# Batch 0's first k load issued as two transfers, and one late row load issued by GpSimd

## The chip, the core and the metric

The kernel runs on one core of a Trainium2 chip. The core has five engines with their own instruction streams: PE (TensorE, matmuls and transposes through a matmul), DVE (VectorE), ACT (ScalarE), POOL (GpSimd) and SP (SyncE, which here only issues DMA transfers). Sixteen DMA engines carry the transfers; SP's transfers stand in one queue (q1 in the profile), GpSimd's in another (q0). The metric is the device time of one execution in microseconds (us).

## What is computed

Linear attention with cosine weights, followed by a gated feed-forward network. There are 8 batches, 8 heads, a sequence of 576 and a head size of 64; the attention's output is read as 4608 tokens of 512 values.

```python
def phi(x, c, s):
    r = np.maximum(x, 0.0)
    return np.concatenate([r * c, r * s], axis=-1)
q_p = phi(q, cos_w, sin_w); k_p = phi(k, cos_w, sin_w)
kv = np.einsum('bhsf,bhsd->bhfd', k_p, v)
z = np.sum(k_p, axis=2)
num = np.einsum('bhsf,bhfd->bhsd', q_p, kv)
den = np.einsum('bhsf,bhf->bhs', q_p, z)[..., None] + 1e-06
x = num / den                              # then laid out as (B * S, H * D)
rms = np.sqrt(np.mean(x * x, axis=-1, keepdims=True) + 1e-06)
xn = x / rms * rms_g
g = xn @ w_gate
out = (g / (1.0 + np.exp(-g)) * (xn @ w_val)) @ w_out
```

## The kernel before

The kernel goes batch by batch. The attention of a batch needs phi(k) and v for `kv` and `z`, then phi(q), transposed, for `num` and `den`; the result `xt` is normalised (`x_sq` squares and sums on ACT, GpSimd takes the power -1/2 into `rs` at L520, `x_norm` on DVE makes `xn` at L527), transposed into `xnT`, and goes through the feed-forward network in blocks of 512 tokens: for each of twelve slices of d_ff four matmuls with `wg` and four with `wv` (L556; in block 0 partly L643 and L658), a SiLU and a product into `hT`, then the matmuls with `wo` (L574). The blocks run in the order 0, 1, 2, 3, 4, 5, 6, 8, 7, where block 8 holds the rows left over from batches 1 to 7. While one block's network runs, the attention of later batches is fitted in between its steps: `at(blk, n, where, f, ...)` puts a call before, inside or after step n of block blk. The order of instructions on each engine is thus the order in which the program writes them; semaphores are placed by a framework.

**Tiles and queues.** Raw q, k and v come into a ring of five buffers named `raw` (L90 to L105). For batches 0 to 2 the rows of k and v lie as 64 x 9 tokens in a half of the partitions for each of two heads, and a dimension `hp` of four head pairs beside them (`kv_rows`). From batch 3 on (`wide`, L75) five tokens lie in a partition and 116 partitions are used. For batch 7 the last partition's row can't be read in one pattern with the others, so `load_kv` loads it separately: a single row, repeated five times, of 40 pieces of 64 values (L118 to L123). SP issues nearly all loads from batch 3 on, the DMA transposes and the output stores. GpSimd issues the loads of the start (q and v of batch 0 in `load_q0` and L213, the weights in L183 and L189) and of batches 1 and 2.

**The start.** SP first issues batch 0's k in two transfers (L149 to L153): tokens 0 to 3 of each partition's nine for all four head pairs (512 pieces of 256 values), then tokens 4 to 8 (512 pieces of 320). ACT issues the small `g4`. GpSimd builds an index table and constants, then issues the first half of q (`load_q0(0)`), v in two halves (`vv0`, L213), the second half of q, then the weights. PE runs ten fillers, matmuls on a zero tile (L598). Then:

```python
    for c in range(NC):
        k_phi(V, 0, c, 0)
        k_phi(A if c < 8 else V, 0, c, 1)
        z0_pe(c)
        if c < NDT:
            g_spread(psC[0], c)
    kv0_pe(0)
    kv0_pe(1)
```

`k_phi` makes phi(k) for token c of all four head pairs (DVE at L294, ACT at L292), `z0_pe` sums its columns on PE (L410), and `kv0_pe(hp)` makes k^T v of head pair hp (L430), which needs `vv0`. After that q is transposed on PE (L363), `kvzs` is copied out (L286, L288), and the chain `nd0_pe`, `nd_post`, `x_sq`, `x_norm`, `x_tr_pe` (L546) leads to the first feed-forward matmuls (L643).

**Semaphores of transfers.** SP's and ACT's transfers take eight semaphores in turn, GpSimd's eight others; a transfer waits until the transfer that used its semaphore before has landed.

Of the kernel before, what the change touches and what calls it, by code (L numbers as in the profile page):

```python
# [17 lines left out]
def kernel(  # L18
# [12 lines left out]
    B, H, S, D = q.shape  # L31
# [4 lines left out]
    HP = H // 2  # L36
    NC = S // 64
# [9 lines left out]
    V, A, G = nc.vector, nc.scalar, nc.gpsimd  # L47
# [22 lines left out]
    def kv_rows(src, b, hps):  # L70
        return src[b, 2 * hps[0] : 2 * hps[1], :, :].rearrange(
            "(hp hh) (s c) d -> (hh s) hp (c d)", hh=2, c=NC
        )

    def wide(b):  # L75
        return b > 2
# [4 lines left out]
    def kv_rows5(src, b, r0, r1):  # L81
        part = src[b, :, 0 : NC5 * (KP - 1), :].rearrange(
            "h (p c) d -> p h (c d)", c=NC5
        )[r0 : min(r1, KP - 1)]
        return bass.AP(part.tensor, part.offset, [[NC5 * D, r1 - r0]] + list(part.ap)[1:])
# [6 lines left out]
    def raw_tile(which, b):  # L92
        if (which, b) not in raw:
            t = ring.tile([P, H * NC5 * D], FP32, name="raw", tag="raw")
            raw[(which, b)] = t
        return raw[(which, b)]

    def raw_kv(which, b):
        t = raw_tile(which, b)
        if wide(b):  # L100
            return t[:, :].rearrange("p (h e) -> p h e", h=H)
        return t[:, 0 : HP * NC * D].rearrange("p (hp e) -> p hp e", hp=HP)
# [4 lines left out]
    def load_kv(which, b, hps=(0, HP), eng=nc.sync):  # L107
        src = k if which == "k" else v
        if not wide(b):
            return eng.dma_start(  # L110
                out=raw_kv(which, b)[:, hps[0] : hps[1], :], in_=kv_rows(src, b, hps)
            )
        last = KP if b < B - 1 else KP - 1
        for r0, r1 in ((0, KM), (KM, last)):
            eng.dma_start(
                out=raw_kv(which, b)[r0:r1, :, :], in_=kv_rows5(src, b, r0, r1)
            )
        if last < KP:  # L118
            eng.dma_start(
                out=raw_kv(which, b)[last:KP, :, :].rearrange("p h (c d) -> p h c d", d=D),  # L120
                in_=src[b, :, S - 1 : S, :].rearrange("h s d -> s h d").unsqueeze(2)
                .to_broadcast([1, H, NC5, D]),
            )  # L123
# [22 lines left out]

    g4 = one.tile([4, P], FP32, name="g4")
    nc.scalar.dma_start(out=g4[:, :], in_=moe_rms_g.rearrange("(t p) -> t p", p=P))
    for c0, c1 in ((0, 4), (4, NC)):  # L149
        nc.sync.dma_start(  # L150
            out=raw_kv("k", 0)[:, :, c0 * D : c1 * D],
            in_=kv_rows(k, 0, (0, HP))[:, :, c0 * D : c1 * D],
        )  # L153


# [67 lines left out]
    for i in range(3):  # L223
        m, e = math.frexp(left)
        part.append(math.ldexp(round(m * 256), e - 8))
        left -= part[i]
        G.memset(eps_rows[32 * i : 32 * i + 32, :], part[i] / 32)
    load_kv("k", 1, eng=G)
    load_w(wg, moe_w_gate, 8, NNT)

    def g_spread(bank, t):
# [12 lines left out]
        out=th[:, 0:NTAB], in0=fidx[:, :], scalar1=S - 1.0, scalar2=ang,  # L244
        op0=ALU.min, op1=ALU.mult,
    )
    for c0, c1, i0, less in ((0, 9, 0, 576.0), (13, 14, 13, 64.0), (19, NTAB, 13, 64.0)):
        V.tensor_scalar(
            out=th[64:128, c0:c1], in0=fidx[64:128, i0 : i0 + c1 - c0],
# [4 lines left out]
        out=th[:, NTAB : 2 * NTAB], in0=th[:, 0:NTAB], scalar1=math.pi / 2.0,  # L254
# [4 lines left out]
        out=sel[:, :, :], in_=ident[0:4, 0:4].unsqueeze(2).to_broadcast([4, NDT, P])  # L259
# [437 lines left out]
    x_sq(0, 1)  # L697
    load_q(1, eng=G)
    load_kv("v", 1, eng=G)
    x_norm(0, 0, (0, HALF))  # L700
    x_norm(0, 0, (HALF, DM))
# [63 lines left out]
    for j in range(4):  # L765
# [3 lines left out]
        if j < 2:  # L769
            at(0, 10 + j, "pe", q_tr_pe, 1, j, bank)  # L770
            at(0, 10 + j, "pre", q_tr_evac, V, 1, j, bank)
    at(0, 8, "post", load_kv, "k", 2, (0, HP), G)
    at(0, 9, "post", v_cast, G, 1, (0, 2))
    at(0, 10, "pre", v_cast, V, 1, (2, 4))
# [184 lines left out]
```

## Time and profile before

| | us |
|---|---|
| median of three runs (322.75, 322.88, 323.72) | 322.88 |
| the profiled execution | 322.91 |
| its span, first to last instruction | 321.1 |
| PE busy | 313.6 |
| DVE busy | 185.4 |
| ACT busy | 165.8 |
| GpSimd (POOL) busy | 40.5 |

The granted clock of PE was 1.0 over the whole span. The DMA engines are busy through most of it: of 40 equal slices the first 29, to 233 us, each have a mean busy share of 0.5 or more. SP's queue carried 41.25 MB, GpSimd's 12.13 MB.

Landing times, median from issue: 5.5 us for the 640 KB of batch 0's k; 6.6 and 8.3 us for the two halves of batch 0's q; 7.2 us for the halves of its v; 13.8 to 20.0 us for groups of weights.

How to read the lines below: in the timeline and in the chain of waits the first two columns are start and length in us; the bracket at the end of a timeline line is the time for which the engine was idle before the instruction and what ended that. In lists of waits the numbers are the total in us, how many, and the longest.

### The profile page before, as it was taken

To read this page: it belongs to the slowest core of one execution; us is meant where nothing else is said; L and a number is where in the kernel's file an instruction comes from. 1 tells how busy PE (TensorE), PEld (TensorE's weight loads), DVE (VectorE), ACT (ScalarE), POOL (GpSimd) and SP (SyncE) were. 2 spreads that over 40 slices of the span, in tenths; PEclk is the share of its full clock that TensorE was granted. 3 is DMA by queue.
4 is the path that set the end of the run, shared out by engine and by line. 5 is a ranking of instruction groups with operands and counts; after the bars stand their busy time and mean duration, and the time that the engine had idled before them with its cause. 6 is when DMAs were issued, how large, how long until landed. Compare 5 with 4: busy or idle time off the path is not lost.

```text
span 321.1 us, 6023 instructions
## 1 busy us (share of the span) xinstructions
PE 313.6 (98%) x2274; PEld 162.4 (51%) x2310; DVE 185.4 (58%) x382; ACT 165.8 (52%) x322; POOL 40.5 (13%) x79
## 2 busy tenths in 40 slices
PE   7999999999999999999999999999999999999996
PEld 2689564544454445444544445544544444444444
DVE  7976977668457773777457644781676034204410
ACT  5766756754574466554744575446543233223321
POOL 9771211002001100010001100100011000000000
PEclk9999999999999999999999999999999999999999
DMA  7999999788999999999799959995522500041002
GB/s 232 239 270 269 282 329 227 201 183 190 223 226 211 187 263 187 221 247 182 162 186 230 197 163 200 197 217 163 99 59 41 116 33 0 0 102 31 1 35 98
DMA packets 80092, 53.76 MB, mean 167 GB/s; under 512 B 52235, under 2 KB 74047, under 8 KB 80063
## 3 DMA queue, kind: packets, MB, share of 16 engines
q1 hardware_dynamic: 73110, 41.25, 62.1%
q0 software_dynamic: 6944, 12.13, 15.5%
q8 instruction: 18, 0.29, 0.4%
q14 instruction: 12, 0.09, 0.1%
q10 hardware_dynamic: 8, 0.00, 0.0%
HBM read 37.83 MB, written 9.44 MB: 147 GB/s over the span
## 4 chain that ended last, share of the span: by engine, by line
PE 94%; DMA 2%; DVE 1%; issue 1%; POOL 1%; ACT 0%; POOLq 0%; ACTq 0%
PE psC L574 27%; PE psV L556 27%; PE psG L556 26%; PE psV L643 2%; PE psA L449 2%; DMA vv<-in_v_dram 2%; PE psG L574 2%; PE psG L643 2%; PE psA L387 2%; PE psA L394 1%; PE psA L474 0%; PE psV L363 0%; PE psG L430 0%; PE psC L546 0%; POOL raw L135 0%
## 5 line engine op out<-in xcount | busy, mean ns | idle before, releaser
L571 DVE TENSOR_TENSOR hT<-psV,sg 128x512 bf16<-128x512 f32 x99 | 68.2, 689 | 96.5 <-PE psV L556 64.1
L556 PE MATMUL psV<-xnT,wv 128*128 128x512 bf16 x344 | 89.6, 379 | 0.7 <-issue 0.2
L570 ACT ACTIVATE sg<-psG 128x512 f32<-128x512 f32 x99 | 58.6, 592 | 60.8 <-PE psG L556 52.7
L556 PE MATMUL psG<-xnT,wg 128*128 128x512 bf16 x337 | 88.5, 379 | 0.7 <-issue 0.2
L574 PE MATMUL psC<-wo,hT 128*128 128x512 bf16 (+1 forms) x400 | 88.4, 376 | 0.4
L574 PEld LDWEIGHTS <-hT 128*128 128x128 bf16 x456 | 43.1, 98 | 47.7
L556 PEld LDWEIGHTS <-wv 128*128 128x128 bf16 x400 | 39.0, 98 | 46.8
L556 PEld LDWEIGHTS <-wg 128*128 128x128 bf16 x400 | 37.0, 98 | 39.9 <-DVE xnT L288 0.2
L520 POOL TENSOR_TENSOR rs<-ms,mhalf 128x1 f32<-128x1 f32 x36 | 20.5, 570 | 193.9 <-ACT scr L515 193.7
L286 ACT COPY osb<-psC 128x512 f32<-128x512 f32 x32 | 18.7, 585 | 49.9 <-PE psC L574 46.1
L515 ACT ACTIVATE scr<-xt 128x513 bf16<-128x513 f32 x36 | 22.8, 635 | 23.3 <-DVE xt L499 22.3
L527 DVE SCALAR_TENSOR_TENSOR xn<-xt,rs,gb 128x512 bf16<-128x512 f32 (+1 forms) x37 | 26.9, 730 | 9.9 <-POOL rs L520 9.9
L292 ACT ACTIVATE kp<-raw,tab 128x256 bf16<-128x256 f32 (+2 forms) x51 | 28.8, 607 | 2.4 <-DMA raw<-in_k_dram 2.4
L499 DVE TENSOR_TENSOR xt<-psA,rec 128x512 f32<-128x512 f32 x36 | 24.9, 691 | 1.2
L292 ACT ACTIVATE qp<-raw,tab 128x512 bf16<-128x512 f32 (+1 forms) x36 | 23.3, 666 | 1.2 <-DMA raw<-in_q_dram 1.1
L294 DVE TENSOR_SCALAR kp<-raw,tab 128x256 bf16<-128x256 f32 (+2 forms) x53 | 20.1, 428 | 0.5 <-DMA raw<-in_k_dram 0.5
L294 DVE TENSOR_SCALAR qp<-raw,tab 128x512 bf16<-128x512 f32 (+1 forms) x34 | 15.3, 463 | 4.7 <-DMA raw<-in_q_dram 4.7
L449 PEld LDWEIGHTS <-qpT 128*128 128x128 bf16 x224 | 10.6, 97 | 6.6
L556 PE MATMUL psV<-xnT_tail,wv 128*128 128x512 bf16 x48 | 12.3, 379 | 0.1
L556 PE MATMUL psG<-xnT_tail,wg 128*128 128x512 bf16 x46 | 12.0, 379 | 0.1
L288 DVE CAST vv<-raw 116x1280 bf16<-116x1280 f32 (+1 forms) x13 | 11.1, 857 | 1.3 <-DMA raw<-in_v_dram 1.3
L449 PE MATMUL psA<-kvzs,qpT 128*128 128x65 bf16 x224 | 11.4, 193 | 0.0
(102 smaller groups left out, 177.7 us busy)
## 6 DMA issues: line engine op xcount, KB each, us to landing
out_dram<-osb SPq DMA_DIRECT2D x27, 256.0 KB, 2.3
raw<-in_q_dram SPq DMA_DIRECT2D x6, 1024.0 KB, 9.1
raw<-in_k_dram SPq DMA_DIRECT2D x5, 1120.0 KB, 8.8
raw<-in_v_dram SPq DMA_DIRECT2D x5, 1120.0 KB, 9.4
raw<-in_k_dram POOLq DMA_DIRECT2D x2, 1152.0 KB, 19.2
raw<-in_v_dram POOLq DMA_DIRECT2D x2, 1152.0 KB, 15.7
out_dram<-osb SPq DMA_DIRECT2D x17, 128.0 KB, 2.6
wg<-in_moe_w_gate_dram POOLq DMA_DIRECT2D x3, 512.0 KB, 13.8
```

The source lines that it names most:

```text
L286: A.copy(out=o, in_=i)
L292: A.activation(out=out_ap, in_=in_ap, func=AF.Relu, scale=scale)
L294: eng.tensor_scalar(out=out_ap, in0=in_ap, scalar1=scale, scalar2=0.0, op0=ALU.mult, op1=ALU.max)
L449: nc.tensor.matmul(heads[:, g, hp, :], lhsT=qpT[:, h, j * P : (j + 1) * P], rhs=kvzs[b][:, g, hp * E : (hp + 1) * E], start=True, stop=True,)
L499: V.tensor_tensor(out=xt[:, 0:DM].rearrange("p (hp g d) -> p g hp d", g=2, d=D), in0=heads[:, :, :, 0:D], in1=rec[:, :, :].unsqueeze(3).to ...
L515: A.activation(out=scr[:, :], in_=xt[:, 0 : DM + 1], func=AF.Square, scale=1.0 / math.sqrt(DM), accum_out=ms[:, :],)
L520: G.tensor_tensor(out=rs[:, :], in0=ms[:, :], in1=mhalf[:, :], op=ALU.pow)
L527: V.scalar_tensor_tensor(out=xn_of[(b, j)][:, c], in0=x_of[(b, j)][:, c], scalar=rs_of[(b, j)][:, :], in1=gb[:, c], op0=ALU.mult, op1=ALU. ...
L556: nc.tensor.matmul(bank[:, cols[0] : cols[1]], lhsT=w[:, t, n * P : (n + 1) * P], rhs=x[:, t, cols[0] : cols[1]], start=(t == 0), stop=(t ...
L570: A.activation(out=sg[:, :], in_=g[:, 0:TB], func=AF.Silu)
L571: V.tensor_tensor(out=hT[:, n, :], in0=v[:, 0:TB], in1=sg[:, :], op=ALU.mult)
L574: nc.tensor.matmul(bank[:, 0 : cols[1] - cols[0]], lhsT=hT[:, n, j * P : (j + 1) * P], rhs=wo[:, n, cols[0] : cols[1]], start=(n == 0), st ...
```

## The change

Batch 0's first k transfer (tokens 0 to 3) becomes two transfers on the same queue, SP's: head pairs 0 and 1, then head pairs 2 and 3, with 256 pieces each. The transfer of tokens 4 to 8 stays as it is, behind them. Users of tokens 0 to 3 wait for both transfers. In `load_kv` the single-row load at the end of batch 7 is issued by GpSimd instead of SP where it is a load of k; that of v stays on SP.

```diff
         if last < KP:
-            eng.dma_start(
+            (G if which == "k" else eng).dma_start(
                 out=raw_kv(which, b)[last:KP, :, :].rearrange("p h (c d) -> p h c d", d=D),
                 in_=src[b, :, S - 1 : S, :].rearrange("h s d -> s h d").unsqueeze(2)
                 .to_broadcast([1, H, NC5, D]),
...
-    for c0, c1 in ((0, 4), (4, NC)):
+    for hps, c0, c1 in (((0, 2), 0, 4), ((2, HP), 0, 4), ((0, HP), 4, NC)):
         nc.sync.dma_start(
-            out=raw_kv("k", 0)[:, :, c0 * D : c1 * D],
-            in_=kv_rows(k, 0, (0, HP))[:, :, c0 * D : c1 * D],
+            out=raw_kv("k", 0)[:, hps[0] : hps[1], c0 * D : c1 * D],
+            in_=kv_rows(k, 0, hps)[:, :, c0 * D : c1 * D],
         )
```

In the built program SP's stream has the two transfers of 256 pieces, then the one of 512. GpSimd's stream has batch 7's row between its 27th and its 28th `rs` of 36, after waits on semaphores of older transfers. The semaphores of SP's transfers stand one place further round from the start to batch 7's k load, and as before from there on. ACT and DVE wait for one more semaphore ahead of their first `k_phi`. The order of PE's, DVE's and ACT's instructions does not change.

## The prediction

> **What bounds the kernel now.** I read the shares of busy time, then the chain of waits, then the first 17 us in order of time, then the DMA queues in short windows. TensorE (PE) is busy 98% of the span, and over the stretch from 16 to 60 us the waits of PE name almost nothing:
>
> ```profile
> PE 313.6 (98%) x2274; PEld 162.4 (51%) x2310; DVE 185.4 (58%) x382; ACT 165.8 (52%) x322; POOL 40.5 (13%) x79
> PE psV L556 <- issue: 0.2, 1, 0.2
> ```
>
> So from about 17 us on nothing but the number of matmuls sets the end, and whatever moves the start of that stretch moves the end by as much. The chain of waits (start, length, what) shows what the start hangs on:
>
> ```profile
> 2.01 1.01 POOL raw L135
> 3.02 6.81 DMA vv<-in_v_dram
> 9.82 0.04 issue
> 9.87 0.71 PE psG L430 x36
> ...
> 12.56 0.43 DVE kvzs L288
> ...
> 16.96 0.28 PE psC L546 x2
> ```
>
> The reader is to see that batch 0's k is not on it. The chain goes through GpSimd's issue of q, then through the first half of batch 0's v (`vv0`), which lands at 3.02 + 6.81 = 9.82; then the k^T v products (L430) start. How near is k? The timeline says:
>
> ```profile
> 0.72 1.01 SPq L150 DMA_DIRECT2D raw<-in_k_dram  x2
> ...
> 5.04 3.42 ACT L292 ACTIVATE kp<-raw,tab 128x256 bf16<-128x256 f32 x8 [2.38 <-DMA raw<-in_k_dram]
> 5.06 3.79 DVE L294 TENSOR_SCALAR kp<-raw,tab 128x256 bf16<-128x256 f32 x10 [0.55 <-DMA raw<-in_k_dram]
> ...
> 8.91 0.39 PE L410 MATMUL psV<-kp,ones 64*128 64x512 bf16 x1
> ...
> 9.87 0.71 PE L430 MATMUL psG<-vv,kp 64*128 64x64 bf16 x36 [0.57 <-DMA vv<-in_v_dram]
> ```
>
> The first k transfer releases ACT and DVE at 5.04, phi(k) ends at 5.06 + 3.79 = 8.85, the column sums (L410) at 8.91 + 0.39 = 9.30, and PE then waits 0.57 us for v. So k has 0.57 us to spare, yet it is not free: both share the DMA engines. The queues' packets in the windows 1.6 to 2.6, 2.6 to 3.4, 3.4 to 5.4 and 5.4 to 6.3 us (q1 is the queue of SP, q0 that of GpSimd; the last two lines are one window; packets, MB, share of 16 engines):
>
> ```profile
> q1 hardware_dynamic: 63, 0.06, 51.1%
> ...
> q1 hardware_dynamic: 199, 0.20, 84.4%
> ...
> q1 hardware_dynamic: 674, 0.78, 108.3%
> ...
> q0 software_dynamic: 51, 0.21, 71.0%
> q1 hardware_dynamic: 120, 0.13, 45.0%
> ```
>
> These are all 1,056 packets of k (512 + 512 pieces, 32 semaphore writes). GpSimd's queue moves nothing before 5.4, although its q was issued at 1.95, and starts as SP's queue runs dry. So v lands when the engines have done k, then q, then v: if k leaves them sooner, v may land sooner. And k starts slowly: 63 packets in the first window against 337 per us (674 in 2.0 us) in the third.
>
> **The change part by part.** The profiled execution took 322.91 us: a span of 321.1 and 1.81 around it. That is 0.03 above the median of the runs (322.88), so I sum against 322.91.
>
> *The first transfer in two.* Bytes and pieces stay (2 x 256 of 1 KB). SP issues one more transfer; its two issues now start 0.52 us apart (0.72 and 1.24), so the second half of k (640 KB) is issued at 1.76 instead of 1.24. That costs nothing while its packets stand behind the first half's: 262 of those 512 were served by 3.4 us, 1.6 us later than the new issue; the first of the second half came at 3.73 in the trace's packet records. Were that cover gone, it would cost up to 0.52. Sixteen more semaphore writes, one per engine, of about 10 ns each in those records: 0.01 us.
>
> The unknown term is the slow start. From the first packet at 1.85 to 3.4 us, 262 packets took 1.55 us; at 337 per us they would have taken 0.78. So at best the cut saves 0.77 us; at worst the queue pauses once for an issue, +0.5. What do rows say of size? The 63rd piece of this load came 1.88 us after its issue; in the four larger k and v loads of some 900 pieces (issued at 66.9, 74.5, 98.4 and 126.6 us) it came after 1.98 to 2.24. About 400 pieces more cost 0.10 to 0.36 us, so 256 fewer might save 0.06 to 0.23. I take -0.2, near the upper of the two since here 16 engines each get 16 pieces instead of 32 before the next transfer feeds them. Both transfers are needed before phi(k) starts, so nothing is won by the first alone.
>
> How much arrives at the end? If q and v follow k without a gap, all of it: phi(k), q, v, the q for j = 2 and 3, and the weights all stand in the same engines' order. If GpSimd's queue could not have begun before 5.4 anyway, none. I take all of the -0.2; the second is a rival.
>
> *One more wait.* ACT and DVE now wait for two transfers before their first phi(k). A semaphore instruction lasts 17 to 28 ns where SP has them (L115). It lies in the 0.57 us that k has to spare: nothing.
>
> *The tiny load.* The last row of batch 7's k, 40 pieces, leaves SP and joins GpSimd's instructions between the 27th and the 28th `rs` (L520):
>
> ```profile
> 183.76 0.55 POOL L520 TENSOR_TENSOR rs<-ms,mhalf 128x1 f32<-128x1 f32 x1 [5.25 <-ACT scr L515]
> 199.85 0.55 POOL L520 TENSOR_TENSOR rs<-ms,mhalf 128x1 f32<-128x1 f32 x1 [15.55 <-ACT scr L515]
> ...
> 195.02 0.80 SPq L119 DMA_DIRECT2D raw<-in_k_dram  x1
> 195.99 1.66 SPq L346 DMA_TRANSPOSE qpT<-qp  x1
> ```
>
> GpSimd idles 15.55 us there. Its issues take 0.74 to 1.08 us (L110, L183, L135), so the load goes out by about 185.4 if its semaphores, those of loads several batches older, are met. Behind it stands only the `rs` at 199.85, then DVE's `xn`. With the slowest landing of a GpSimd load on the page, 20.0 us, it is there by 205.4; phi of batch 7 starts at 213.43. Nothing. Without the cover, each us past 199.85 would hold back `rs`, and DVE behind it. SP gains 0.97 us (195.02 to 195.99) for the transposes behind it, but PE waits for none of them: nothing. From the start to there, SP's transfers use the semaphore one place further round the eight; each still waits for the transfer eight before it: nothing.
>
> **Sum:** -0.2 + 0.01 + 0 = -0.19, rounded -0.2; 322.91 - 0.2 = 322.7 us.
>
> **The rivals.**
>
> *A. GpSimd's queue is not ready before 5.4.* For it: no packet of q0 sooner, 2.4 us after its issue ended at 3.02. Against: its start falls just when SP's queue runs dry. Then v lands at 9.82 as before: 322.9.
>
> *B. The whole slow start goes.* With engines fed in half the time, the 0.77 us vanish, and the first packet comes sooner too: it comes 1.13 us after the issue here, and 0.84 after the issue of an output store of 128 pieces. -0.77 - 0.29 = -1.06: 321.85. For it: the engines' share is 51% and 84% where it could be 100%. Against: the weak dependence on size above, and some first packets last 0.4 to 0.8 us, which looks like memory and not supply.
>
> *C. GpSimd's q slips between k's pieces (slower).* The second half of k is issued 0.52 us later; should GpSimd's packets come first or by turns, its 640 KB, which took some 1.9 us (4.4 to 6.3), would take twice that and land near 8.6 instead of 1.24 + 5.5 = 6.74. Six of DVE's ten phi(k) (0.38 us each) follow, 2.3 us, and then the last column sums, 0.45 us (8.85 to 9.30): 11.35, where L430 starts at 9.87 now. +1.5: 324.4. It decides once that half lands after 7.1 (9.87 - 0.45 - 2.3). For it: q0 has work issued from 1.95 on. Against: it did not slip in at the boundary between the two transfers before.
> The Trainium skill ("DMA: Bandwidth & Descriptors", Queues, rings and completion order) has each engine take turns between the queues that have work, packet by packet. By that rule C is what happens as soon as q0 is ready before k is through; the trace has no such turn before 5.4, so by the rule q0 was not ready, which speaks for A.
>
> *D. Each transfer pays its fixed part in line (slower).* Issue to first packet is 1.13 us and last packet to release about 0.5 (4.52 to 5.04); a third transfer paying them over again lands k's second half 1.6 later, at 8.35: L430 at 11.1, +1.2: 324.1. Against: the second transfer's packets now begin while the first's still run, at 389 GB/s without a gap.
> The Trainium skill (same page, Anatomy of one DMA) gives a fixed cost of about 2.0 us per transfer on GpSimd's path; paid in line it would add an estimated 2.0 to the landing. The trace disagrees for SP's queue: 640 KB landed 1.7 us after the 512 KB released their users.
>
> *E. PE falls to half pace (slower).* The first fillers (512 columns) follow each other 0.42 to 0.43 us apart until about 4.5 us, L410's matmuls of as many columns at 8.02 to 8.9 us 0.22 apart. If a longer gap before 17 us brought that pace back for the same 3.3 us, it costs 1.65: 324.6. Against: PE's longest wait once started is 0.6 us, and the forecast shortens the first one.
>
> **How the numbers follow.** Forecast 0.36, A 0.16, B 0.26, C 0.12, D 0.04, E 0.06. About 0.3% (1 us) is what a measurement of this kernel can tell from no change. Forecast and A are within it: 0.52; B is faster: 0.26; C, D and E are slower: 0.22. The likeliest gives 322.7, its own range 322.2 to 323.3 (from 322.91, the bounds -0.77 and +0.5 of the slow start, each drawn in by 0.1). To hold 8 in 10 the range reaches to B on one side and towards C on the other: 321.7 to 324.3.
>
> **What would show it.** Right: ACT's first phi(k) at about 4.85, v landing and the first L430 near 9.65, more than 63 packets in 1.6 to 2.6; GpSimd's L119 near 184.3. A: k earlier, L430 still at 9.87. B: phi(k) near 4.0. C: packets of q0 before q1 is through, and DVE waiting for k between its phi(k). E: L643 twice as long from 17 us. Wrong altogether: any new wait of PE after 30 us, above all behind `xn` near 200 us.

## The result, and the profile after

The changed kernel takes 327.4 us (median of 5 runs, 327.02 to 327.89), the kernel before 323.06 us beside it (5 runs, 322.75 to 326.27): a ratio of 1.0113, with a 95% interval of 1.0065 to 1.0162. The change makes the kernel slower by some 4.3 us. The forecast was 322.7 us (321.7 to 324.3).

The profiled execution took 327.09 us with a span of 325.28 (before: 322.91 and 321.13), so the 4.15 us lie inside the span. From the page of the changed kernel, first the shares of busy time, then a line of the 40 slices:

```profile
PE 318.6 (98%) x2310; PEld 164.1 (50%) x2310; DVE 185.2 (57%) x382; ACT 165.7 (51%) x322; POOL 40.7 (13%) x80
...
PEclk9599999999999999999999999999999999999999
```

PE is busy for 318.6 us instead of 313.6, with the same instructions (2310 records against 2274: some matmuls are missing from the trace of the kernel before, as both have 2310 weight loads), and in the second slice (8 to 16 us) it was granted half its clock. That is where to look. The chain of waits of the changed kernel, in the first 14 us (start, length, what):

```profile
1.73 8.34 DMA raw<-in_k_dram
10.07 0.02 issue
10.09 0.52 ACT kp L292
10.61 0.04 issue
10.65 0.58 PE psC L410
...
12.97 0.97 PE psG L430 x36
```

Before, the chain went through v. Now it goes through k, and only one of its three transfers: the third, issued at 1.73, lands at 10.07. The timeline of the changed kernel shows both sides of the change:

```profile
0.72 1.48 SPq L150 DMA_DIRECT2D raw<-in_k_dram  x3
...
4.50 1.71 ACT L292 ACTIVATE kp<-raw,tab 128x256 bf16<-128x256 f32 x4 [1.83 <-DMA raw<-in_k_dram]
4.52 1.60 DVE L294 TENSOR_SCALAR kp<-raw,tab 128x256 bf16<-128x256 f32 x4
...
10.09 1.71 ACT L292 ACTIVATE kp<-raw,tab 128x256 bf16<-128x256 f32 x4 [3.89 <-DMA raw<-in_k_dram]
10.09 1.66 DVE L294 TENSOR_SCALAR kp<-raw,tab 128x256 bf16<-128x256 f32 x6 [3.98 <-DMA raw<-in_k_dram]
...
10.65 0.58 PE L410 MATMUL psC<-kp,ones 64*128 64x512 bf16 x1 [2.60 <-ACT kp L292]
...
12.74 1.21 PE L430 MATMUL psG<-vv,kp 64*128 64x64 bf16 x36
```

The halves did what they were cut for: phi(k) begins at 4.50 instead of 5.04. But ACT and DVE, which went through all of k in one stretch before, stop after tokens 0 to 3 and wait 3.89 and 3.98 us for tokens 4 to 8. PE stands still for 2.60 us, and L430 starts at 12.74 instead of 9.87. Where the packets were can be read from the DMA queues in the windows 1.6 to 2.6, 2.6 to 3.4, 4.0 to 5.1, 6.3 to 7.5 and 7.5 to 9.7 us of the changed kernel (packets, MB, share of 16 engines):

```profile
q1 hardware_dynamic: 110, 0.11, 52.7%
...
q1 hardware_dynamic: 315, 0.31, 108.7%
...
q1 hardware_dynamic: 112, 0.14, 71.9%
...
q0 software_dynamic: 78, 0.32, 72.8%
q1 hardware_dynamic: 56, 0.07, 15.7%
...
q0 software_dynamic: 275, 0.37, 85.1%
q1 hardware_dynamic: 174, 0.21, 28.4%
```

The same query over 4.0 to 5.1 us of the kernel before:

```profile
q1 hardware_dynamic: 359, 0.43, 107.4%
```

In the first two windows the changed kernel is ahead: 110 and 315 packets against 63 and 199. Its first 512 pieces end at 3.96 us in the packet records, against 4.52. Then, where the kernel before goes on at full pace, SP's queue falls to a third, 0.14 MB in 1.1 us instead of 0.43. From 6.3 us most of the engines' time goes to GpSimd's q and v. By the semaphores, to which each of the sixteen engines adds one when its share is done, eight engines finish their share of the third transfer between 5.97 and 7.12, about as before (6.02 to 6.74); the other eight only between 9.03 and 10.07.

PE's pace, from windows of the changed kernel (length, then busy time and instructions of PE, PEld, DVE, ACT, POOL; then PE's granted clock, DMA share, GB/s):

```profile
10.00:12.70 2.70, 2.05 (x10) 0.96 (x12) 2.61 (x9) 2.61 (x7) 1.12 (x4) 0.50 1.15 291
12.70:16.00 3.30, 3.30 (x64) 2.96 (x60) 2.15 (x5) 1.35 (x4) 1.74 (x3) 0.50 1.23 216
16.00:21.50 5.50, 5.40 (x100) 3.64 (x98) 4.43 (x12) 4.59 (x12) 2.41 (x4) 1.00 1.24 207
```

By the clock's records PE is at half clock from 9.15 to 15.97, for 6.83 us: this begins while PE still waits (8.05 to 10.65), and goes on for 5.3 us behind the wait. The first feed-forward matmul (L643) starts at 21.49 instead of 17.31. So the account is: L430 later by 2.87; from L430 to L643 8.75 us instead of 7.44, another 1.31; from L643 to the end 303.79 instead of 303.82. Together 2.87 + 1.31 - 0.03 = 4.15, the whole difference.

The moved row, on GpSimd in the changed kernel:

```profile
187.94 0.55 POOL L520 TENSOR_TENSOR rs<-ms,mhalf 128x1 f32<-128x1 f32 x1 [5.25 <-ACT scr L515]
188.62 0.64 POOL L119 DMA_DIRECT2D raw<-in_k_dram  x1
204.04 0.56 POOL L520 TENSOR_TENSOR rs<-ms,mhalf 128x1 f32<-128x1 f32 x1 [14.79 <-ACT scr L515]
```

It is issued 0.1 us after the `rs` ahead of it ends, and GpSimd still idles 14.79 us behind it.

### The profile page after: what moved, and what is told of

The parts are those of the page before. It is cut to its first block, busy times and chain, and to the rows that moved or that the text cites. A ratio compares the mean times of both kernels' runs of the same rounds, so it can differ in the third digit from the quotient of the medians.

```text
span 325.3 us, 6063 instructions
## 1 busy us (share of the span) xinstructions
PE 318.6 (98%) x2310; PEld 164.1 (50%) x2310; DVE 185.2 (57%) x382; ACT 165.7 (51%) x322; POOL 40.7 (13%) x80
## 4 chain that ended last, share of the span: by engine, by line
PE 94%; DMA 3%; ACT 1%; SPq 0%; DVE 0%; POOL 0%; issue 0%; ACTq 0%
PE psC L574 27%; PE psV L556 27%; PE psG L556 27%; DMA raw<-in_k_dram 3%; PE psV L643 2%; PE psA L449 2%; PE psG L574 2%; PE psG L643 2%; PE psA L387 2%; PE psA L394 1%; PE psC L410 1%; PE psV L363 1%; ACT qp L292 0%; PE psA L474 0%; PE psC L546 0%; ACT qpT L286 0%
## 5 line engine op out<-in xcount | busy, mean ns | idle before, releaser
L556 PE MATMUL psG<-xnT,wg 128*128 128x512 bf16 x352 | 90.3, 379 | 0.0
L294 DVE TENSOR_SCALAR qp<-raw,tab 128x512 bf16<-128x512 f32 (+1 forms) x34 | 16.3, 492 | 4.3 <-DMA raw<-in_q_dram 4.3
(103 smaller groups left out, 184.3 us busy)
```

Source lines behind the costliest of these rows:

```text
L294: eng.tensor_scalar(out=out_ap, in0=in_ap, scalar1=scale, scalar2=0.0, op0=ALU.mult, op1=ALU.max)
L556: nc.tensor.matmul(bank[:, cols[0] : cols[1]], lhsT=w[:, t, n * P : (n + 1) * P], rhs=x[:, t, cols[0] : cols[1]], start=(t == 0), stop=(t ...
```

## The experiments

Times are medians. The kernel before was run beside each group and took 323.0 (24 runs), 323.2 (32 runs) and 323.18 (15 runs) for the three groups that follow. Each diff is an excerpt. It is against the kernel before, but for `gap_filled` and `gpsimd_late`, where it shows what is added to the changed kernel; where only the head of the loop over k's transfers is shown, the lines under it are those of the change. In `split_only`, `tiny_first` and `tiny_mid` the row of batch 7 stays on SP; in all others GpSimd issues it as in the change, which only the diff of `row_only` shows.

### The two parts alone, and a third transfer that is not a split

`split_only`: the split without the row.

```diff
-    for c0, c1 in ((0, 4), (4, NC)):
+    for hps, c0, c1 in (((0, 2), 0, 4), ((2, HP), 0, 4), ((0, HP), 4, NC)):
```

> The first k load in two, batch 7's row left on SP's queue. If the split is the cause (theory 1): as slow as the changed kernel, 326.5 to 328, the second half of k (tokens 4 to 8) landing near 10 us, phi(k) of token 4 starting near 10 and PE's clock halved in one stretch before 17 us. If the moved row is the cause, or its shift of the semaphores' order (rival): near 323, phi(k) without a stop in the middle.

Measured: 326.76 us, ratio 1.0115 (1.0096 to 1.0134). The timeline of `split_only` has the same break:

```profile
4.29 1.71 ACT L292 ACTIVATE kp<-raw,tab 128x256 bf16<-128x256 f32 x4 [1.63 <-DMA raw<-in_k_dram]
...
9.67 1.71 ACT L292 ACTIVATE kp<-raw,tab 128x256 bf16<-128x256 f32 x4 [3.67 <-DMA raw<-in_k_dram]
```

The split alone makes the loss.

`row_only`: the row on GpSimd without the split.

```diff
-            eng.dma_start(
+            (G if which == "k" else eng).dma_start(
```

> Only batch 7's row moved to GpSimd. Theory 1: no change, 322.7 to 323.5, since GpSimd idles 15 us there. Rival (the row is the cause): 326 to 328.

Measured: 323.23 us, ratio 1.001 (0.9998 to 1.0023). The row is worth nothing that can be measured.

`tiny_first` and `tiny_mid`: k's two transfers as before, with a load of 2 KB that nothing uses issued by SP ahead of both, or between them. In each, k's last transfer is the third in SP's queue and is issued about 0.5 us later than before, as in the change.

```diff
+    gx = one.tile([4, P], FP32, name="gx")
+    nc.sync.dma_start(out=gx[:, :], in_=moe_rms_g.rearrange("(t p) -> t p", p=P))
     for c0, c1 in ((0, 4), (4, NC)):
```

> The kernel before, with one more load of 2 KB that nobody uses issued on SP's queue ahead of k's two. Three transfers on the queue, the last issued 0.5 us later, as in the changed kernel, but a transfer of 512 pieces stands right ahead of the last. Theory 2a (the third transfer, or its later issue, is what starves the last one): the last lands near 10 us, 326 to 328. Theory 2b (the last transfer starves because the short ones ahead of it end before its pieces are ready): its start is covered until about 4.3 us, k lands about 0.5 later than before (5.5 and 7.3), 323 to 323.9.

> The same 2 KB load issued between k's two transfers. The last transfer is third and 0.5 us later, with 512 pieces ahead of it. Theory 2a: it lands near 10 us, 326 to 328. Theory 2b: covered until about 3.7 us, as before; lands by 7, 322.7 to 323.6.

Measured: `tiny_first` 324.08 us, ratio 1.0037 (1.0016 to 1.0059); `tiny_mid` 323.14 us, ratio 1.0005 (0.9993 to 1.0016). In neither does phi(k) stop between tokens 3 and 4: in `tiny_first`, whose time is just above what was expected, all of k comes about 0.45 later (landings end at 5.39 and 7.18), in `tiny_mid` its last part lands by 6.45. A third transfer, or one issued 0.5 us later, does not by itself starve.

### The wait, the half clock and GpSimd's queue

`late_half_act`: the split, with k's last transfer issued by ACT on its own queue, so that SP issues only two.

```diff
-    for c0, c1 in ((0, 4), (4, NC)):
-        nc.sync.dma_start(
+    for hps, c0, c1 in (((0, 2), 0, 4), ((2, HP), 0, 4), ((0, HP), 4, NC)):
+        (nc.sync if c0 == 0 else nc.scalar).dma_start(
```

> The changed kernel with k's last transfer (tokens 4 to 8) issued by ACT, whose queue is otherwise empty, at about 1.3 us. Theory 2b (on half of the DMA engines the last transfer isn't ready when the short ones ahead of it end): on a queue of its own it is ready in time, phi(k) starts near 4.5 and goes on without a stop, v lands sooner: 322.2 to 323. Rival (one source makes the pieces for SP's and ACT's transfers, one after the other, and falls behind all the same): phi(k) of token 4 waits beyond 8 us, 325 to 328.

Measured: 323.38 us, ratio 0.9997 (0.9984 to 1.001). The loss is gone, and so is the gain at the start, so the time misses the 322.2 to 323 of its theory: phi(k) begins at 5.06 again, and k's last part lands by 6.32. The two queues share the engines, so the halves no longer come early.

`gap_filled`: the change (its three transfers), and twelve idle matmuls on PE after token 3's column sums, so that PE does not stand still while it waits for k.

```diff
+        if c == 3:
+            filler(12, psV[0])
```

> The changed kernel with twelve more fillers on PE (2.6 us at full pace) after the column sums of token 3, where PE waits for k. Nothing else is touched, so k^T v starts as late as in the changed kernel (12.7). Theory: of the 4.2 us lost, 2.9 are the late k and some 1.3 PE's half pace after its 2.6 us gap; with the gap filled the clock stays at 1.0 and 0.9 to 1.4 come back: 326.0 to 326.5. Rival (the other engines, not PE's pace, set the rest): 327.2 to 327.6.

Measured: 325.13 us, ratio 1.0052 (1.0037 to 1.0068). Windows of `gap_filled`, columns as above:

```profile
10.00:12.00 2.00, 1.76 (x16) 0.76 (x17) 2.00 (x9) 2.00 (x6) 0.76 (x1) 1.00 1.14 303
12.00:16.00 4.00, 4.00 (x116) 3.21 (x113) 3.68 (x10) 3.83 (x9) 3.18 (x5) 1.00 1.22 222
```

The clock stays at 1.0, and L430 to L643 takes 7.50 us, as before (7.44), instead of 8.75. The column sums between k's landing and L430 gain too: 9.74 to 11.93 is 2.19 us, in the changed kernel 10.09 to 12.74 is 2.65. So half clock costs 1.25 + 0.46 = 1.7 of the 4.15 us; the rest is the late k. It came out faster than expected because the expectation had left out those 0.46, and k landed 0.35 earlier here.

`gpsimd_late`: the change, with three memsets of a tile that nothing uses ahead of GpSimd's first load, so that its q, v and weights are issued 1.7 to 1.8 us later (q at 3.76 instead of 1.96).

```diff
+    pad = one.tile([P, TB], FP32, name="pad")
+    for i in range(3):
+        G.memset(pad[:, :], 0.0)
```

> The changed kernel with three clears of an unused tile on GpSimd ahead of its first load, so that q, v and the weights are issued some 2 us later. Theory 3a (GpSimd's q takes the engines on which k's last transfer came late, and k stands behind it): with q away, k's last transfer lands by about 6 us, and v about 2 us later than before sets the start: 324 to 326. Theory 3b (k's pieces themselves aren't there on half of the engines, whoever else wants them): it still lands after 8 us, and the time is 327 or more.

Measured: 325.91 us, ratio 1.0077 (1.0049 to 1.0104); v is late now, as GpSimd issues it later, and the time says little. What it tells is k. From `gpsimd_late`, the queue of SP in 4.0 to 5.1 us:

```profile
q1 hardware_dynamic: 137, 0.17, 76.6%
```

and ACT's phi(k) in its timeline (the lines of the code stand three further down in this kernel):

```profile
4.48 1.70 ACT L295 ACTIVATE kp<-raw,tab 128x256 bf16<-128x256 f32 x4 [1.13 <-DMA raw<-in_k_dram]
...
7.34 1.70 ACT L295 ACTIVATE kp<-raw,tab 128x256 bf16<-128x256 f32 x4 [1.15 <-DMA raw<-in_k_dram]
```

SP's queue is as thin as in the changed kernel, 0.17 MB in 1.1 us where the kernel before moved 0.43, with no packet of GpSimd's queue before 5.62. So the lack of packets is the queue's own, and not GpSimd's doing. But all sixteen engines now finish k between 5.99 and 7.32, later than theory 3a had it and well before the 8 us of 3b. The thin stretch alone costs 7.32 - 6.74 = 0.58 us in these two profiles (0.87 against the 6.45 of `row_only`); the other 2.75, to 10.07, appear only where GpSimd's q is there to be taken up first.

`split_late`: the first transfer whole, the second cut in two halves of the head pairs.

```diff
-    for c0, c1 in ((0, 4), (4, NC)):
+    for hps, c0, c1 in (((0, HP), 0, 4), ((0, 2), 4, NC), ((2, HP), 4, NC)):
```

> The first k transfer whole again (512 pieces), the second (tokens 4 to 8) in two of 256. Three transfers, the last one short. Theory 2b: 512 pieces cover the wait, nothing starves, phi(k) as in the kernel before: 322.6 to 323.5. Rival (a transfer of 256 pieces, or cutting k at all, is what disturbs the queue): 325 to 328.

Measured: 323.11 us, ratio 0.9993 (0.9978 to 1.0008). Three transfers of the same bytes, one after the other on SP, and no loss: cutting as such is harmless.

### How much must lie ahead

`four_parts`: both transfers cut in two, so that the third is half as large.

```diff
+    for hps, c0, c1 in (((0, 2), 0, 4), ((2, HP), 0, 4), ((0, 2), 4, NC), ((2, HP), 4, NC)):
```

> Both k transfers in two: four transfers of 256 pieces on SP's queue, issued 0.5 us apart. Theory 4a (a transfer of 256 pieces is there in full some 0.7 us after its first piece, one of 512 only after 1.4 or more): the third keeps the engines fed when the second ends near 3.9, no DMA engine runs dry, k's last tokens land by 6.7: 322.8 to 324. Theory 4b (what matters is that the transfer issued third isn't ready by 3.9, whatever its size): GpSimd's q takes engines again, phi(k) of token 4 waits beyond 8 us: 325.5 to 328.

Measured: 326.94 us (2 runs), ratio 1.0119 (1.0071 to 1.0167). The timeline of `four_parts`:

```profile
4.47 1.70 ACT L292 ACTIVATE kp<-raw,tab 128x256 bf16<-128x256 f32 x4 [1.81 <-DMA raw<-in_k_dram]
...
9.84 1.71 ACT L292 ACTIVATE kp<-raw,tab 128x256 bf16<-128x256 f32 x4 [3.66 <-DMA raw<-in_k_dram]
```

As bad as the change: the size of the late transfer is not what makes it late.

`small_then_large` and `large_then_small`: tokens 0 to 3 cut unevenly, one head pair (128 pieces) and then three (384), or the other way round.

```diff
+    for hps, c0, c1 in (((0, 1), 0, 4), ((1, HP), 0, 4), ((0, HP), 4, NC)):
...
+    for hps, c0, c1 in (((0, 3), 0, 4), ((3, HP), 0, 4), ((0, HP), 4, NC)):
```

> The first k transfer in 128 and 384 pieces instead of 256 and 256. Theory 5a (the transfer right ahead has to cover the next one's start, 384 pieces do it longer): less starved or not at all, 323 to 325. Theory 5b (only the 512 pieces ahead in total count, and how soon they are done): as the changed kernel, 326 to 328.

> 384 and then 128 pieces. Theory 5a: only 128 pieces stand right ahead of the last transfer: starved as in the changed kernel or more, 326.5 to 329. Theory 5b: 326 to 328 as well; if the first of 384 starts as slowly as one of 512, the pieces ahead end later, near 4.2, and it is less: 323 to 326.

Measured: `small_then_large` 323.64 us, ratio 1.0009 (0.9996 to 1.0021); `large_then_small` 325.12 us, ratio 1.0057 (1.003 to 1.0084), its runs spread from 323.16 to 326.24. SP's queue in 4.0 to 5.1 us, first in `small_then_large`:

```profile
q1 hardware_dynamic: 320, 0.40, 100.7%
```

and in `large_then_small`, with the start of tokens 4 to 8 on ACT:

```profile
q1 hardware_dynamic: 291, 0.37, 93.6%
...
8.56 1.70 ACT L292 ACTIVATE kp<-raw,tab 128x256 bf16<-128x256 f32 x4 [1.97 <-DMA raw<-in_k_dram]
```

The same three issues and the same pieces give no loss, a part of it or all of it, in step with how long the pieces ahead last. The semaphores make a table of it (when the pieces ahead of k's last part are done, first to last engine; then how many engines finish the last part after 7.2 us; the trace does not name the engines, so these are counts):

| kernel | pieces ahead done, us | engines late |
|---|---|---|
| split_only | 3.87 to 4.18 | 8 |
| the change | 3.94 to 4.39 | 8 |
| gap_filled | 3.98 to 4.28 | 10 |
| four_parts | 3.92 to 4.36 | 3 with the third, 9 with the fourth |
| large_then_small | 4.13 to 4.34, one 4.77 | 3 |
| tiny_mid | 4.09 to 4.54 | 0 |
| small_then_large | 4.11 to 4.56 | 0 |
| before (second of two transfers) | 4.21 to 4.95 | 0 |
| tiny_first | 4.42 to 5.39 | 0 |

The ranges overlap, and each row is one execution: the table shows a trend, not a sharp limit. The profiled run of `small_then_large`, the slowest of its eight (324.22), lost time elsewhere: its k was whole at 6.63, but v landed at 11.11 instead of 9.82, and L430 waited for it until 11.15. Whether the cut has a part in that is open.

`large_in_middle`: the large transfer between the two halves.

```diff
+    for hps, c0, c1 in (((0, 2), 0, 4), ((0, HP), 4, NC), ((2, HP), 0, 4)):
```

> The changed kernel's three transfers in another order: 256 pieces of tokens 0 to 3, the 512 of tokens 4 to 8, the other 256. The large one is issued second, at 1.24, but has only 256 pieces ahead of it, done near 3.2. Theory 4b (being third is what is late): no starving, the pieces run without a gap, phi(k) starts near 6.3 with all of k there: 323.5 to 324.8. Theory 4a: the large one isn't there in full when the first ends, the queue is slow from 3.2 to 4.5 and GpSimd's q, ready near 4.5, takes some engines: phi(k) beyond 7, 325 or more.

Measured: 327.58 us (2 runs), ratio 1.0139 (1.0082 to 1.0195), a miss. All of k landed by 6.92 and no engine was lost to GpSimd's q, as expected of it. But phi(k) can start only at 7.03, when the last transfer is in, and its price was put far too low. The PE timeline of `large_in_middle`:

```profile
1.18 4.45 PE L598 MATMUL psC<-warm 128*128 128x512 bf16 x10 [1.18 <-DVE warm L164]
7.66 0.60 PE L410 MATMUL psC<-kp,ones 64*128 64x512 bf16 x1 [2.03 <-DVE kp L294]
...
13.64 1.18 PE L430 MATMUL psG<-vv,kp 64*128 64x64 bf16 x36
```

The fillers are over at 5.63, PE waits 2.03 us, and every column sum takes 0.60 us instead of 0.39: PE stayed at half pace until 16.75 us, where the first record of a full clock stands (4.4 us in the kernel before). L430 comes 3.77 us later than before and the span is 5.14 longer: here the wait on PE cost more than its length.

## Why the prediction was wrong

The step that failed is the issue of the third transfer: "That costs nothing while its packets stand behind the first half's: 262 of those 512 were served by 3.4 us ... Were that cover gone, it would cost up to 0.52." Two things were wrong with it. The cover was read from the kernel before, while the very next term of the sum took some of it away: with a quick start 409 of the 512 pieces had begun by 3.4 us (the 425 packets less 16 semaphore writes), not 262, and the pieces ahead ended at 3.96 instead of 4.52. And the price without cover was worth more than the delay of the issue: the landing moved from 6.74 to 10.07, by 3.33 us. The 0.52 comes near the price of the thin queue alone (0.58 in `gpsimd_late`), but by luck, since it is the delay of an issue and not the length of a thin stretch; the other 2.75 came from the second queue, which takes engines that have run dry. Two terms of one sum were not allowed to meet.

- *What bounds the kernel.* v by 0.57 us ahead of k was right. "Whatever moves the start of that stretch moves the end by as much" held for the delay (L643 4.18 later, end 4.15 later). For a gain it is not shown: in `row_only`, `tiny_mid` and `split_late` L643 came 0.38 to 0.42 earlier than in the profile of before, and the span was not shorter (321.32, 321.26 and 321.18 against 321.13). Even a forecast gain that arrived might have been given back later, but these are single executions, and runs of one kernel differ by 1 us and more.
- *The slow start, -0.2.* The direction was right and the size somewhat too small: against the one profile of before the 512 pieces ended 0.56 earlier and phi(k) began 0.54 earlier, inside the bounds of -0.77 and +0.5. Over all profiles it is less: by the packet records the 512 pieces end between 3.82 and 4.05 in the five kernels that cut them in two halves ahead of k's last part on SP's queue, and between 4.08 and 4.52 in the four that issue them first and whole, 0.36 earlier on average.
- *"All of it arrives at the end".* None did; the gain was what uncovered the third transfer.
- *One more wait, 0; the tiny load, 0.* Both right. L119 was forecast for 184.3 and came at 188.62, which is the shift of the whole kernel by 4.2; `row_only` measures the row at 1.001 (0.9998 to 1.0023).
- *Rival A* (GpSimd's queue not ready before 5.4) is refuted: with the same issue its first packet came at 4.43 in `gap_filled` and 4.57 in `split_only`. In the changed kernel itself it came at 5.12, so this too varies between executions.
- *Rival B* (the whole slow start goes): the start went part of the way (phi(k) at 4.50, where B had 4.0), the time did not follow.
- *Rival C* (GpSimd's q slips between k's pieces) is what happened. Its formula holds: a landing at 10.07 + 2.3 + 0.45 gives 12.82, and L430 came at 12.74. Its landing of 8.6 was too early: it let the queues take turns from 4.4 us on at full pace, and not with a thin queue on engines that had run dry.
- *Rival D* (the fixed part paid in line) does not say it: the third transfer's first packet came at 3.56, with the pieces ahead still running, and `split_late` pays nothing for its third transfer.
- *Rival E* (half pace after a longer gap, +1.65) happened as well, behind C: 1.31 after L430, and about 1.7 with the column sums. C and E were priced and given chances as separate cases; C makes the gap that E needs, and together they are 1.5 + 1.65 = 3.15 by the forecast's own numbers, outside its range.

What the runs settle: the split is the cause. Where most engines are done with the pieces ahead by about 4.1 to 4.2 us, the third transfer's packets come thinly until about 5 us, and GpSimd's q, whose first packets then come between 4.43 and 5.12, takes part of the engines, whose share of k waits 2 to 3 us; where the pieces ahead last longer, nothing is lost. That the engines that finish late are those that took up q is read from the counts and from `gpsimd_late`, as the trace does not name the engines. The wait then costs PE its clock. What stays open is why the third transfer is thin at first. Its packets also take longer then: 113 ns on average in 4.0 to 5.1 us (112 packets in 71.9% of the engines' time) against 53 in the kernel before. Those of the first transfer do so at the very start (130 ns on average in 1.6 to 2.6 us of the kernel before), but no run here separates a slow supply of packets from slow first reads. No version tried beats the kernel before: `split_late`, `late_half_act` and `tiny_mid` are the same as it.

The Trainium skill ("DMA: Bandwidth & Descriptors", Queues, rings and completion order) says that an engine takes turns between the queues that have work, a whole packet, of several pieces, at a time. The trace agrees from 6.3 us on in so far as both queues move (78 and 56 packets, then 275 and 174); whose turn it was is not in it. It does not show it earlier: in the kernel before GpSimd's queue had no piece before 5.44, though with the same issue it was ready by 4.43 in `gap_filled`. In the eight kernels whose engines stay busy with k from 4.0 to 5.1 us, the first packet of GpSimd's queue comes between 5.23 and 5.70, each time 0.4 to 0.6 us before the first engine reports its share of k as done. In the kernel before a report comes 0.48 us after a last packet (6.26 to 6.74), so that is about when an engine runs out of k. So here the engines kept to the queue of k (SP's, in `late_half_act` also ACT's) while it still fed them.

## What to carry to other kernels

A cover that is named for a cost has to be read in the schedule that the change makes, not in the old one: if another term of the same sum shortens the cover, work out both together. Here the second queue did no harm while the urgent one always had packets ready, and took engines when it had not; cut a transfer so that the pieces ahead outlast the first moments of the one behind (128 then 384 pieces did here, 256 then 256 did not). And where a rival makes PE wait early in the kernel, price a stretch of half clock in the same case.

## What was not expected of the hardware

PE was throttled by waits shorter than the half-clock stretches that followed: a wait of 2.60 us brought 6.83 us at half clock in the changed kernel, and one of 2.02 us brought 3.41 us in `split_only`. The Trainium skill ("TensorE: Matmul & The Clock Gate", What's actually happening) gives an idle window of about 3.4 us before the clock is halved, and one window of work before it is restored. The lengths agree, 3.41 and twice 3.41, though in the changed kernel the clock came back only after two; and idle times of 2.0 and 2.6 us were enough to halve it.

The length of the wait alone does not decide it. First two lines of PE in `large_then_small`, then one in `small_then_large`:

```profile
9.12 0.37 PE L410 MATMUL psC<-kp,ones 64*128 64x512 bf16 x1 [0.72 <-ACT kp L292]
...
11.12 1.21 PE L430 MATMUL psG<-vv,kp 64*128 64x64 bf16 x36
...
11.15 0.71 PE L430 MATMUL psG<-vv,kp 64*128 64x64 bf16 x36 [1.82 <-DMA vv<-in_v_dram]
```

After a wait of only 0.72 us the first kernel was at half clock from 10.05 to 13.46; after one of 1.82 us the second stayed at 1.0. What decides it is open.

The start itself varies between executions by about as much as the change was to bring: `row_only` and the kernel before issue the same first loads at the same times, and phi(k) begins at 4.73 and 5.04 on ACT. A single run of `tiny_mid` took 328.12 us with a mean clock of 0.989, the clock of the changed kernel, where its other seven took 322.81 to 323.53. It was not profiled, so whether the third transfer starved there, with pieces ahead that ended at 4.09 to 4.54 in the profiled run, is open. The kernel before has such a run too: one of its 32 in the second group took 325.44 us with the same mean clock of 0.989.
